# Twelve consecutive tokens per partition instead of every 128th: a new on-chip token order for a fused attention and MLP kernel

## The chip, the cores and the metric

The kernel runs on one core of a Trainium2 chip. Times are device microseconds (us) of one execution. The profile of an execution gives its own span, from the first to the last instruction, and its granted TensorE clock.

## The reference

The inputs are `u` and `v` of shape (8, 3008, 256), `z` of shape (8, 3008, 64), and two weights, all in float32. What is computed, cut to what matters:

```python
scores = (1.0 / S) * np.matmul(z, z.transpose(0, 2, 1))   # per batch, S = 3008
attn = np.maximum(scores, 0.0) ** 2
x = (u * np.matmul(attn, v)).reshape(B * S, D)            # B = 8, D = 256
h = x @ w_in                                              # d_ff = 2048
out = (h * np.cos(h)) @ w_out                             # float32, (24064, 256)
```

There is no mask and no position: every token of a batch meets every other token of it. A kernel may therefore hold the tokens of a batch in any order on chip, as long as `z`, `v`, `u` and `out` use the same one.

## The kernel before

**Tiles.** A batch of 3008 tokens is 23 blocks of 128 tokens and a tail of 64. Six groups (`NC = 6`) of four blocks make the unit of work, a *slot*; there are 8 x 6 = 48 slots. The blocks also fall into two halves of 12 blocks (`halves`), the second being 11 full blocks and the tail. Block `k` has its token number `p` on partition `p`: partition `p` holds tokens `p`, `128 + p`, `256 + p` and so on.

**Loads.** `load_z` brings half a batch of `z` into `z16` with a cast to fp16, twice side by side (`h` = 0, 1; lines 118 and 124). `load_rows` (line 140, and line 146 for the tail) brings four blocks of `v` or `u` with a cast to fp16. These are issued from GpSimd (POOL). For batch 0, `z` comes in float32 through six DMAs issued from SyncE and ScalarE (line 633, tail 639), is cast on VectorE and GpSimd (`cast_z`, line 645), turned on TensorE (`turn_on_pe`, line 649) and copied to `zT` (`copy_turned`). For the later batches, `turn_z` (line 133), and for every slot `turn_u` (line 160), turn the tiles by a transposing DMA on SyncE's queue. Weights come by two more GpSimd DMAs (lines 708 and 712).

**Work of a slot.** `phase_a(s)` multiplies the 24 score blocks by `v` (`emit_value`, line 258), in halves of the width: 23 blocks with `dh = 0`, the tail, 23 blocks with `dh = 1`; block `k` reads `vs[b, k // 4]`. Scores of later slots are made in between (`emit_score`, line 194), pass ScalarE (line 204) and VectorE (lines 209, 212), and their mirror images are made by transposing DMAs on SyncE's queue (`emit_turns`, lines 238 and 244). `gate_mul` (line 286) multiplies by `uT`. `phase_b(s)` alternates the first MLP product of slot `s - 1` (`emit_h`, line 404; cosine on ScalarE, line 412; product on VectorE, line 415) with the second one of slot `s - 2` (`product`, line 482, for all but the first and last slot; sums on GpSimd, lines 433, 434, 504, 507).

**Stores.** `store_half` writes two blocks of `out` with one DMA on SyncE's queue (line 547; lines 543 to 545 where the tails of two batches share a block). `last_y` makes the last slot's output block by block (line 525), copies it on ScalarE (line 572) and stores it (lines 578, 580, 581).

**Order.** The program is in `manual_schedule`: every engine executes in the order of the Python code. Batch `b + 1` has its `v` group 0 loaded in the slot `J = 4` of batch `b`, and groups 1 to 5 in the slot `J = 5`, after that slot's `phase_a`, since `v` has seven buffers and the last pass over the old groups must be done. At the start, seven matmuls on zeros (line 664) run before the first `z` block is turned.

Of the kernel before, what the change touches and what calls it, by code (L numbers as in the profile page):

```python
# [14 lines left out]
def kernel(  # L15
# [9 lines left out]
    nc = tc.nc  # L25
# [3 lines left out]
    B, S, D = u.shape  # L29
    dqk = z.shape[2]  # L30
    Dff = moe_w_in.shape[1]
    P = 128
    H = P // 2
    CW = 512
    NB = (S + P - 1) // P
    NC = (S + CW - 1) // CW
    WL = S - (NC - 1) * CW
    NFT = Dff // P
    NSLOT = B * NC
    NPC = 18  # L40
    assert D == 2 * P and dqk == H and S - (NB - 1) * P == H and NB == 4 * NC
    assert B % 2 == 0 and WL == 3 * P + H and NFT == 16

    inv_s2 = (1.0 / float(S)) * (1.0 / float(S))
    half_pi = float(math.pi / 2.0)
# [62 lines left out]
    halves = [(0, NB // 2), (NB // 2, NB)]  # L108
    z16s, zTs, vs, u16s, uTs, xs, gs = {}, {}, {}, {}, {}, {}, {}
    yps = {}  # L110

    def load_z(b, half):
        lo, hi = halves[half]
        z16 = zpool.tile([P, NB // 2, P], FP16, name="z16")
        z16s[b] = z16
        full = min(hi, NB - 1)
        for h in range(2):
            nc.gpsimd.dma_start(
                z16[:, 0:full - lo, h * dqk:(h + 1) * dqk],
                z[b, lo * P:full * P, :].rearrange("(j p) d -> p j d", p=P),  # L120
            )
            if hi == NB:
                for r in range(2):
                    nc.gpsimd.dma_start(
                        z16[r * H:(r + 1) * H, hi - lo - 1, h * dqk:(h + 1) * dqk],
                        z[b, (NB - 1) * P:S, :],
                    )
# [10 lines left out]
    def load_rows(t, src, b, g):  # L138
        full = 4 if g < NC - 1 else 3
        nc.gpsimd.dma_start(  # L140
            t[:, 0:full, :],
            src[b, g * CW:g * CW + full * P, :].rearrange("(j p) d -> p j d", p=P),
        )
        if full == 3:
            for r in range(2):
                nc.gpsimd.dma_start(t[r * H:(r + 1) * H, 3, :], src[b, S - H:S, :])

    def load_v(b, g):
        t = vpool.tile([P, 4, D], FP16, name="v16")
        load_rows(t, v, b, g)  # L150
        vs[b, g] = t

    def load_u(s):
        t = upool.tile([P, 4, D], FP16, name="u16")
        load_rows(t, u, s // NC, s % NC)
        u16s[s] = t
# [237 lines left out]
    def mwidth(m):  # L394
        return 3 * P if m % (2 * NC) == NC - 1 else CW
# [27 lines left out]
    T = 2 * P  # L423
# [41 lines left out]
    def product(m, n, place):  # L465
# [34 lines left out]
        if n in (1, 5):  # L500
            nc.scalar.activation(parts[n], acc, AF.Copy, bias=0.0, scale=inv_s2)
        elif n == 6:
            add(parts[6], parts[1])
            nc.gpsimd.tensor_tensor(c12, parts[6], parts[5], ALU.add)
        elif n == 7:
            add(c21, parts[6])
            nc.gpsimd.tensor_tensor(c22, c21, parts[5], ALU.add)
        elif n == 2:
            add(c11, parts[1])
        elif n == 3:  # L510
            add(c12, c12)
            store_half(m, 0, y_outs[m][0])
        else:
            add(c21, c21)
            store_half(m, 1, y_outs[m][1])

    def y_bank(m, k):
        if m == NSLOT - 1 and k == 3:
            return E[0][:, 0, 0:D]
        bank = 1 - k // 2 if m == NSLOT - 1 else k // 2  # L520
        return M[bank][:, (k % 2) * D:(k % 2 + 1) * D]

    def y_block(m, ft, k):
        final = m == NSLOT - 1
        nc.tensor.matmul(  # L525
            y_bank(m, k),
            gs[m][:, ft, k * P:(k + 1) * P],
            w_out16[:, ft, :],
            start=(ft == 0 and (k % 2 == 0 or (final and k == 3))),
            stop=(ft == NFT - 1 and (k % 2 == 1 or k == mwidth(m) // P - 1 or (final and k == 2))),  # L530
        )

    def emit_y(m, i):
        for ft in range(2 * i, 2 * i + 2):
            for k in range(mwidth(m) // P):
                y_block(m, ft, k)

    def store_half(m, half, o):
        b, J = m // NC, m % NC
        n = min(2, mwidth(m) // P - 2 * half)  # L540
        t0 = b * S + J * CW + half * T
        if J == NC - 1 and half == 1 and n == 2:
            nc.sync.dma_start(out[t0:t0 + P, :], o[:, 0, :])
            nc.sync.dma_start(out[t0 + P:t0 + P + H, :], o[0:H, 1, :])
            nc.sync.dma_start(out[b * S - H:b * S, :], o[H:P, 1, :])
        else:
            nc.sync.dma_start(
                out[t0:t0 + n * P, :].rearrange("(k p) d -> p k d", p=P), o[:, 0:n, :]
            )

    def store_y(m):
        for half in range(2):
            n = min(2, mwidth(m) // P - 2 * half)
            o = opool.tile([P, 2, D], FP32, name="o")
            nc.scalar.activation(
                o[:, 0:n, :],
                M[half].rearrange("p (k d) -> p k d", d=D)[:, 0:n, :],
                AF.Copy, bias=0.0, scale=inv_s2,
            )
            store_half(m, half, o)  # L560

    def last_y(m):
        b, J = m // NC, m % NC
        for ft in range(NFT):
            y_block(m, ft, 0)
            y_block(m, ft, 1)
        for k in range(4):
            if k >= 2:
                for ft in range(NFT):
                    y_block(m, ft, k)  # L570
            o = opool.tile([P, 2, D], FP32, name="o")
            nc.scalar.activation(
                o[:, 0, :], y_bank(m, k),
                AF.Copy, bias=0.0, scale=inv_s2,
            )
            t0 = b * S + J * CW + k * P
            if k < 3:
                nc.sync.dma_start(out[t0:t0 + P, :], o[:, 0, :])
            else:
                nc.sync.dma_start(out[t0:t0 + H, :], o[0:H, 0, :])  # L580
                nc.scalar.dma_start(out[b * S - H:b * S, :], o[H:P, 0, :])

    def phase_b(s):
# [46 lines left out]
    for g in range(NC):  # L630
        eng = nc.sync if g % 2 == 0 else nc.scalar
        full = 4 if g < NC - 1 else 3
        eng.dma_start(
            z32[g][:, 0:full, :],
            z[0, g * CW:g * CW + full * P, :].rearrange("(j p) d -> p j d", p=P),
        )
        if full == 3:
            for r in range(2):
                nc.sync.dma_start(z32[g][r * H:(r + 1) * H, 3, :], z[0, S - H:S, :])
# [78 lines left out]
    turn_u(3)  # L718
    load_u(4)
    load_z(1, 0)  # L720
    mix_weights()
    phase_b(2)
    turn_z(1, 0)
    load_z(1, 1)
    turn_u(4)

    for s in range(3, NSLOT + 1):
        b, J = s // NC, s % NC
        if s < NSLOT - 2:
            load_u(s + 2)  # L730
        if b > 0 and J == 2 and b + 1 < B:
            load_z(b + 1, 1)
        if s < NSLOT:
            phase_a(s)
        if b + 1 < B:
            if b > 0 and J == 0:
                load_z(b + 1, 0)
            if b > 0 and J == 1:
                turn_z(b + 1, 0)
            if J == (2 if b > 0 else 3):  # L740
                turn_z(b + 1, 1)
            if J == NC - 2:
                load_v(b + 1, 0)
            if J == NC - 1:
                for g in range(1, NC):
                    load_v(b + 1, g)
        if s < NSLOT - 2:
            turn_u(s + 2)
        phase_b(s)
    last_y(NSLOT - 1)  # L750


# [28 lines left out]
```

## Time and profile before

| What | us |
|---|---|
| Median of 3 runs (1192.8 to 1193.27) | 1193.12 |
| The profiled execution's own time | 1193.15 |
| Its span | 1191.4 |
| TensorE busy | 1183.3 |
| VectorE busy | 1012.3 |
| ScalarE busy | 794.9 |
| GpSimd busy | 690.5 |

A busy figure counts instructions in execution; for TensorE it includes the modelled overlap of pipelined matmuls. The queue that GpSimd fills ("software") carried 97440 packets and 32.78 MB and took 27.3% of 16 DMA engines' span; the queue of SyncE ("hardware", q1) carried 380752 packets and 112.93 MB and took 54.4%. In all there were 479862 packets, 404208 of them under 512 B. The granted clock was 0.999 of full speed. A line such as "v<-in_v_dram POOLq DMA_DIRECT2D x40, 256.0 KB, 8.8" reads: 40 DMAs of 256 KB each, with a median of 8.8 us from issue to landing.

### The profile page before, as it was taken

How to read it: one execution, taken by the hardware profiler on the slowest of the kernel's cores; microseconds unless marked ns; L12 is line 12 of the kernel's file. 1: busy time of each engine (PE TensorE's matmuls, PEld its weight loads, DVE VectorE, ACT ScalarE, POOL GpSimd, SP SyncE). 2: the span in 40 equal slices, each digit the busy share in tenths (PEclk: the TensorE clock that was granted, in tenths of full speed). 3: DMA queues.
4: the chain of work that ended last, by engine and by line, in shares of the span. 5: the costliest groups of instructions: out<-in, count | busy, mean ns of one | idle time of the engine just before them, and what ended most of it. 6: DMA issues, size and time to landing. Idle time of an engine off the chain costs nothing.

```text
span 1191.4 us, 29044 instructions
## 1 busy us (share of the span) xinstructions
PE 1183.3 (99%) x11887; PEld 727.2 (61%) x11887; DVE 1012.3 (85%) x1302; ACT 794.9 (67%) x927; POOL 690.5 (58%) x717
## 2 busy tenths in 40 slices
PE   9999999999999999999999999999999999999998
PEld 4556665665566656666566665656666566665566
DVE  6899888889988898888988889888888888888776
ACT  7966676667666676667676676666766666666454
POOL 3287746657466573755647556476565665545452
PEclk9999999999999999999999999999999999999999
DMA  9999998569995699946999459973898737964301
GB/s 160 172 170 163 138 147 131 102 121 134 143 130 98 123 140 162 131 84 104 157 147 135 85 104 161 169 119 72 122 164 149 122 71 123 166 125 86 65 20 54
DMA packets 479862, 148.00 MB, mean 124 GB/s; under 512 B 404208, under 2 KB 479472, under 8 KB 479728
## 3 DMA queue, kind: packets, MB, share of 16 engines
q1 hardware_dynamic: 380752, 112.93, 54.4%
q0 software_dynamic: 97440, 32.78, 27.3%
q8 instruction: 93, 1.52, 0.5%
q10 hardware_dynamic: 1536, 0.43, 0.2%
q14 instruction: 41, 0.34, 0.1%
HBM read 66.32 MB, written 24.64 MB: 76 GB/s over the span
## 4 chain that ended last, share of the span: by engine, by line
PE 97%; ACT 1%; DVE 1%; issue 0%; POOL 0%; DVEq 0%; ACTq 0%
PE E L404 27%; PE M L482 23%; PE M L258 20%; PE E L258 19%; PE E L194 5%; PE M L525 1%; ACT r L204 1%; PE M L460 1%; DVE g L415 0%; PE E L664 0%; DVE sm L270 0%; PE E L525 0%; POOL s L433 0%; ACT c L412 0%; DVE o L495 0%
## 5 line engine op out<-in xcount | busy, mean ns | idle before, releaser
L412 ACT ACTIVATE c<-E 128x1024 f16<-128x1024 f32 (+1 forms) x384 | 385.7, 1007 | 216.4 <-PE E L404 214.1
L415 DVE SCALAR_TENSOR_TENSOR g<-E,c 128x1024 f16<-128x1024 f32 (+1 forms) x384 | 458.4, 1195 | 60.6 <-ACT c L412 59.5
L204 ACT ACTIVATE r<-E 128x512 f16<-128x512 f32 (+1 forms) x342 | 327.9, 967 | 112.7 <-PE E L194 106.5
L258 PEld LDWEIGHTS <-v 64*128 64x128 f16 x4512 | 246.3, 94 | 229.3 <-issue 19.4
L404 PE MATMUL E<-x,w_in 128*128 128x512 f16 (+1 forms) x1408 | 354.0, 375 | 0.0
L433 POOL TENSOR_TENSOR s<-g 128x512 f16<-128x512 f16 (+1 forms) x184 | 208.3, 1132 | 188.5 <-DVE g L415 138.7
L258 PE MATMUL M<-A,v 64*128 64x512 f16 (+1 forms) x2256 | 283.0, 372 | 0.2 <-DVE o L495 0.2
L258 PE MATMUL E<-A,v 64*128 64x512 f16 (+1 forms) x2256 | 278.1, 371 | 0.0
L434 POOL TENSOR_TENSOR g<-g 128x512 f16<-128x512 f16 (+1 forms) x184 | 219.5, 1193 | 14.4
L404 PEld LDWEIGHTS <-w_in 128*128 128x128 f16 x1536 | 133.1, 98 | 108.9 <-issue 19.5
L482 PEld LDWEIGHTS <-g 128*128 128x128 f16 x2816 | 172.5, 98 | 40.8
L209 DVE TENSOR_TENSOR A<-r 128x1024 f16<-128x1024 f16 x240 | 174.0, 737 | 15.0 <-ACT r L204 14.3
L286 POOL TENSOR_TENSOR x<-sm,uT 128x512 f16<-128x512 f32 (+1 forms) x43 | 48.6, 1132 | 212.9 <-DVE sm L270 212.5
L482 PEld LDWEIGHTS <-s 128*128 128x128 f16 x2112 | 129.4, 98 | 32.1 <-DVE s L440 0.5
L194 PE MATMUL E<-zT 64*128 64x512 f16 (+4 forms) x684 | 127.6, 355 | 2.0 <-DVE sm L270 0.7
L440 DVE TENSOR_TENSOR s<-s,g 128x1024 f16<-128x1024 f16 (+1 forms) x92 | 100.6, 1094 | 2.1 <-POOL s L433 2.1
L482 PE MATMUL M<-w_mix,s 128*128 128x128 f16 x1408 | 94.0, 219 | 0.3 <-POOL s L433 0.3
L482 PE MATMUL M<-w_mix,g 128*128 128x128 f16 x1408 | 93.6, 219 | 0.0
L482 PE MATMUL M<-w_out,g 128*128 128x128 f16 x1408 | 93.6, 219 | 0.0
L212 DVE TENSOR_TENSOR A<-r 128x512 f16<-128x512 f16 (+1 forms) x102 | 79.6, 781 | 8.9 <-ACT r L204 8.1
L194 PEld LDWEIGHTS <-zT 64*128 64x128 f16 x684 | 38.8, 94 | 38.5 <-issue 4.0
L442 DVE TENSOR_TENSOR s<-g,s 128x1024 f16<-128x1024 f16 (+1 forms) x92 | 60.5, 660 | 0.0
(58 smaller groups left out, 646.9 us busy)
## 6 DMA issues: line engine op xcount, KB each, us to landing
out_dram<-o SPq DMA_DIRECT2D x87, 256.0 KB, 2.2
v<-in_v_dram POOLq DMA_DIRECT2D x40, 256.0 KB, 8.8
u<-in_u_dram POOLq DMA_DIRECT2D x40, 256.0 KB, 4.8
A<-A SPq DMA_TRANSPOSE x252, 5.1
z<-in_z_dram POOLq DMA_DIRECT2D x14, 192.0 KB, 10.6
z<-in_z_dram POOLq DMA_DIRECT2D x14, 176.0 KB, 5.9
v<-in_v_dram POOLq DMA_DIRECT2D x8, 192.0 KB, 11.9
u<-in_u_dram POOLq DMA_DIRECT2D x8, 192.0 KB, 4.1
```

Source lines behind the costliest of these rows:

```text
L194: nc.tensor.matmul(e[:, t, 0:Wt], zT[rows, k * P:(k + 1) * P], zT[rows, J * CW:J * CW + Wt], start=True, stop=True,)
L204: nc.scalar.activation(r[:, :, 0:W], e[:, :, 0:W], AF.Relu)
L209: nc.vector.tensor_tensor(a4, r4, r4, ALU.mult)
L212: nc.vector.tensor_tensor(a4, r[:, :, 0:W], r[:, :, 0:W], ALU.mult)
L258: nc.tensor.matmul(bank[:, 0:width(J)], vs[b, k // 4][t * H:(t + 1) * H, k % 4, dh * P:(dh + 1) * P], value_rhs(b, J, k, t), start=start, ...
L404: nc.tensor.matmul(e[:, f, 0:W], w_in16[:, k, ft * P:(ft + 1) * P], x[:, k, 0:W], start=(k == 0), stop=(k == 1),)
L412: nc.scalar.activation(c[:, :, 0:W], e[:, :, 0:W], AF.Sin, bias=half_pi, scale=inv_s2)
L415: return lambda: nc.vector.scalar_tensor_tensor(gs[m][:, 2 * i:2 * i + 2, 0:W], e[:, :, 0:W], 1.0, c[:, :, 0:W], ALU.mult, ALU.mult)
L433: nc.gpsimd.tensor_tensor(s1[:, f, 0:n], g[:, f, low], g[:, lower, low], ALU.add)
L434: nc.gpsimd.tensor_tensor(g[:, f, low], g[:, f, up], g[:, f, low], ALU.subtract)
L440: nc.vector.tensor_tensor(s2[:, f, 0:n], s1[:, f, 0:n], g[:, f, up], ALU.subtract)
L482: nc.tensor.matmul(acc[:, k * P:(k + 1) * P], left[:, ft, k * P:(k + 1) * P], right[:, ft, :], start=(ft == 0 and k == 0), stop=(ft == F - ...
```

## The change

The order of the tokens on chip changes within each half of a batch. The first half's 1536 tokens lie twelve to a partition: partition `p` holds tokens `12 p` to `12 p + 11`, and block `k` is the `k`-th of these on every partition. The second half's 1408 tokens lie eleven to a partition, and the tail of 64 stays as it was. `z`, `v`, `u` and `out` all follow the new order through two helpers. The number of DMAs, their bytes, the tiles in SBUF and every compute instruction stay the same; the address patterns on the DRAM side differ. In DRAM, a partition's four blocks of `v` or `u` are now 4 KB in one piece (3 KB in the last group), the twelve of `z` 3 KB, the four of batch 0's `z` 1 KB, and two blocks of `out` 2 KB. Where `last_y` stores one block, its 128 rows of 1 KB were adjacent and now stand 11 KB apart; the stores of tails are the same.

```diff
-    assert B % 2 == 0 and WL == 3 * P + H and NFT == 16
+    assert NC == 6 and B % 2 == 0 and WL == 3 * P + H and NFT == 16
...
+    def half_rows(rows, half):
+        lo, hi = halves[half]
+        n = min(hi, NB - 1) - lo
+        return rows[lo * P:(lo + n) * P, :].rearrange("(p j) d -> p j d", p=P)
+
+    def group_rows(rows, g):
+        first = 4 * (g % 3)
+        return half_rows(rows, g // 3)[:, first:first + (4 if g < NC - 1 else 3), :]
+
     def load_z(b, half):
...
-                z16[:, 0:full - lo, h * dqk:(h + 1) * dqk],
-                z[b, lo * P:full * P, :].rearrange("(j p) d -> p j d", p=P),
+                z16[:, 0:n, h * dqk:(h + 1) * dqk], half_rows(z[b], half)
...
     def load_rows(t, src, b, g):
         nc.gpsimd.dma_start(
             t[:, 0:full, :],
-            src[b, g * CW:g * CW + full * P, :].rearrange("(j p) d -> p j d", p=P),
+            group_rows(src[b], g),
         )
...
+    def out_rows(m):
+        b, J = m // NC, m % NC
+        return group_rows(out[b * S:(b + 1) * S, :], J)
+
     def store_half(m, half, o):
...
-            nc.sync.dma_start(out[t0:t0 + P, :], o[:, 0, :])
-            nc.sync.dma_start(out[t0 + P:t0 + P + H, :], o[0:H, 1, :])
+            nc.sync.dma_start(rows[:, 2, :], o[:, 0, :])
+            nc.sync.dma_start(out[(b + 1) * S - H:(b + 1) * S, :], o[0:H, 1, :])
             nc.sync.dma_start(out[b * S - H:b * S, :], o[H:P, 1, :])
         else:
-            nc.sync.dma_start(
-                out[t0:t0 + n * P, :].rearrange("(k p) d -> p k d", p=P), o[:, 0:n, :]
-            )
+            nc.sync.dma_start(rows[:, 2 * half:2 * half + n, :], o[:, 0:n, :])
...
     def last_y(m):
             if k < 3:
-                nc.sync.dma_start(out[t0:t0 + P, :], o[:, 0, :])
+                nc.sync.dma_start(out_rows(m)[:, k, :], o[:, 0, :])
             else:
-                nc.sync.dma_start(out[t0:t0 + H, :], o[0:H, 0, :])
+                nc.sync.dma_start(out[(b + 1) * S - H:(b + 1) * S, :], o[0:H, 0, :])
...
         eng.dma_start(
             z32[g][:, 0:full, :],
-            z[0, g * CW:g * CW + full * P, :].rearrange("(j p) d -> p j d", p=P),
+            group_rows(z[0], g),
         )
```

More of the change, by code (lines that the diff above doesn't have):

```diff
@@ L115, in load_z @@
         z16s[b] = z16
-        full = min(hi, NB - 1)
+        n = min(hi, NB - 1) - lo
         for h in range(2):
             nc.gpsimd.dma_start(
-                z16[:, 0:full - lo, h * dqk:(h + 1) * dqk],
-                z[b, lo * P:full * P, :].rearrange("(j p) d -> p j d", p=P),
+                z16[:, 0:n, h * dqk:(h + 1) * dqk], half_rows(z[b], half)
             )
@@ L536, in emit_y @@
                 y_block(m, ft, k)
+    def out_rows(m):
+        b, J = m // NC, m % NC
+        return group_rows(out[b * S:(b + 1) * S, :], J)
     def store_half(m, half, o):
-        b, J = m // NC, m % NC
+        b = m // NC
+        rows = out_rows(m)
         n = min(2, mwidth(m) // P - 2 * half)
-        t0 = b * S + J * CW + half * T
-        if J == NC - 1 and half == 1 and n == 2:
-            nc.sync.dma_start(out[t0:t0 + P, :], o[:, 0, :])
-            nc.sync.dma_start(out[t0 + P:t0 + P + H, :], o[0:H, 1, :])
+        if m % NC == NC - 1 and half == 1 and n == 2:
+            nc.sync.dma_start(rows[:, 2, :], o[:, 0, :])
+            nc.sync.dma_start(out[(b + 1) * S - H:(b + 1) * S, :], o[0:H, 1, :])
             nc.sync.dma_start(out[b * S - H:b * S, :], o[H:P, 1, :])
         else:
-            nc.sync.dma_start(
-                out[t0:t0 + n * P, :].rearrange("(k p) d -> p k d", p=P), o[:, 0:n, :]
-            )
+            nc.sync.dma_start(rows[:, 2 * half:2 * half + n, :], o[:, 0:n, :])
     def store_y(m):
@@ L575, in last_y @@
             )
-            t0 = b * S + J * CW + k * P
             if k < 3:
-                nc.sync.dma_start(out[t0:t0 + P, :], o[:, 0, :])
+                nc.sync.dma_start(out_rows(m)[:, k, :], o[:, 0, :])
             else:
-                nc.sync.dma_start(out[t0:t0 + H, :], o[0:H, 0, :])
+                nc.sync.dma_start(out[(b + 1) * S - H:(b + 1) * S, :], o[0:H, 0, :])
                 nc.scalar.dma_start(out[b * S - H:b * S, :], o[H:P, 0, :])
```

## The prediction

> **What bounds the kernel now.** I read the page's busy table and slices first:
>
> ```profile
> PE 1183.3 (99%) x11887; PEld 727.2 (61%) x11887; DVE 1012.3 (85%) x1302; ACT 794.9 (67%) x927; POOL 690.5 (58%) x717
> ...
> PE   9999999999999999999999999999999999999998
> ...
> DMA  9999998569995699946999459973898737964301
> ```
>
> TensorE (PE) is never short of work, and the DMA engines, at nine tenths in many slices, are not idle either. A busy PE need not be a PE at its peak, so the chain of work that ended last comes next:
>
> ```profile
> PE 97%; ACT 1%; DVE 1%; issue 0%; POOL 0%; DVEq 0%; ACTq 0%
> PE E L404 27%; PE M L482 23%; PE M L258 20%; PE E L258 19%; PE E L194 5%; PE M L525 1%; ACT r L204 1%; PE M L460 1%; DVE g L415 0%; PE E L664 0%; DVE sm L270 0%; PE E L525 0%; POOL s L433 0%; ACT c L412 0%; DVE o L495 0%
> ```
>
> 97% of the end time is matmuls one after the other; no DMA stands in it. In the chain's pieces, 8 matmuls of line 404 take 1.73 us (216 ns each) and 16 of line 258 the same 1.73 us (216 ns for a pair on the two 64-row halves). The waits of PE alone, all eight of them:
>
> ```profile
> PE E L664 <- DVE s L627: 1.2, 1, 1.2
> PE E L194 <- DVE sm L270: 0.7, 1, 0.7
> PE E L194 <- DVE g L415: 0.4, 1, 0.4
> PE E L194 <- ACT zT L657: 0.4, 1, 0.4
> PE M L482 <- POOL s L433: 0.3, 1, 0.3
> PE E L194 <- DVE zT L659: 0.2, 1, 0.2
> PE M L258 <- DVE o L495: 0.2, 1, 0.2
> PE E L194 <- ACT r L204: 0.2, 1, 0.2
> ```
>
> They sum to 3.6 us and none was ended by a DMA. So I forecast from three places where a transfer could still reach the end: the start-up, the tightest load of the interior, and the last stores.
>
> **What the Trainium skill says.** "TensorE: Matmul & The Clock Gate", section "Back-to-back issue gap", gives N/2.4 + 2.5 ns for one matmul at full clock: 216 ns for 512 columns. The trace agrees (216 ns), so PE streams at its rate and earlier data can't speed it up. "DMA: Bandwidth & Descriptors", section "Specifications", asks for rows of at least 512 B, and "Why small descriptors are slow (HBM only)" names a fixed cost per packet; the two weight loads, equal in bytes, point that way:
>
> ```profile
> w_in<-in_moe_w_in_dram POOLq DMA_DIRECT2D x1, 1024.0 KB, 11.0
> w_out<-in_moe_w_out_dram POOLq DMA_DIRECT2D x1, 1024.0 KB, 14.9
> ```
>
> The first moves in rows of 8 KB, the second in rows of 1 KB; what ran beside them differs, so it is a hint only. "Issuing engines are not separate DMA queues" says that all queues share the 16 engines. The trace agrees: two transposes of line 244 issued at 273.09 us, beside the loads of `v`, kept SyncE's queue 12.45 us, while three at 323.83, with few loads about, took 8.40.
>
> **The change, part by part.** No compute instruction and no DMA is added or taken away: 11887 matmuls at the same durations. What changes is how a DMA is cut.
>
> *Packets.* I expect one packet for each piece that is contiguous on both sides. A load of `v` or `u` goes from 512 packets (128 partitions x 4) to 128; with the 8 shorter ones of each tensor, 47104 rows become 12288. Two-block stores go from 256 to 128 (87 x 128 = 11136 fewer). Batch 0's `z` loses 2208. The later `z` keeps its 128-byte pieces, because its destination has gaps. 479862 packets become about 431700, and GpSimd's queue goes from 97440 to about 62600. The transposes, most of q1, stay.
>
> *Issue on POOL.* 96 loads at 751 to 817 ns (line 140). The nearest rows with fewer pieces are the tail loads (64 pieces, about 550 ns) and `w_in` (256 pieces, 751 ns), so each is worth 0 to 0.27 us, at most 26 us of POOL. POOL is 58% busy and in the steady part PE waits for it once, 0.3 us: priced at 0, up to -0.3 if that wait goes. Cover: VectorE's 85% and PE's own stream.
>
> *Start-up.* The first six loads of `z` land in 3.7 to 6.4 us. With 1 KB rows, I take 1 us less. The chain's start says what that is worth:
>
> ```profile
> 0.86 0.28 DVE s L627
> 1.14 0.04 issue
> 1.19 3.17 PE E L664 x7
> 4.35 0.04 issue
> 4.39 0.52 PE turned L649 x4
> ```
>
> VectorE has the first `z` at 3.91 and ends its cast at about 4.31, but PE is busy with seven matmuls on zeros until 4.36 and takes up the block at 4.39. At most 0.03 us can go there; what is late next is the zeros' end, which doesn't move. The later casts end at 5.97, 8.23 and 9.24 us, and PE reaches those blocks in its own order at 6.35, 9.61 and 11.13, after work that waits for ScalarE. Earlier casts bring nothing; they may cost something, since GpSimd's casts and issues slide under other VectorE work. Bounds: -0.3 to +0.3 us; I take -0.1.
>
> *Loads in the interior.* The tightest is `v` of the last batch, five big loads and two tails:
>
> ```profile
> L140 POOL DMA_DIRECT2D v<-in_v_dram x5: 740/742/746, 1007.2 to 1011.3; - x5
> L146 POOL DMA_DIRECT2D v<-in_v_dram x2: 539/548/558, 1012.1 to 1012.6; - x2
> ...
> DMA to landing us min/median/max: 11.1/15.4/16.1
> ```
>
> Group 5, the last big one, is issued at 1011.3 and lands 16.1 us later, at 1027.4. PE starts the slot's value products at 1024.17 and reaches block 20, group 5's first, after 40 matmuls and three score pairs, at 1029.15. That is a margin of 1.7 us. The same sum gives 3.6 us for batch 4 (tails), 4.1 for batch 2, 4.4 for batch 6, and over 7 for the odd batches. Earlier landing widens these margins and moves PE by 0. `z` and `u` have more: `u` is turned two slots ahead. The transposes of scores are queued on SyncE behind `u`'s and `z`'s turns; I matched the order of emission to the queue, and those near the `v` burst (285.68 to 289.66, line 238) serve a slot a whole 24.5 us later. Gain 0.
>
> *Stores.* Issue on SyncE's queue is 345 to 372 ns either way; 2.2 us to landing may fall. They wait for VectorE, nobody but the last slot waits for them. There, ScalarE waits 1.5 us for two stores to free a buffer, but its last copy starts at 1187.10, 0.04 us after PE's last matmul, so that wait is covered. The final two stores are tails and unchanged. The three single-block stores keep 128 packets of 1 KB, now 11 KB apart instead of adjacent; the trace has no such store. Bounds: 0, since the last (issued 1186.2, some 1.7 us to land) ends before the tails' 1189.7, to +1 us if scattered rows took twice as long. I take 0.
>
> *Sum:* 1193.15 (this execution, 0.03 above the median) - 0.1 + 0 + 0 + 0, about **1193.0**.
>
> **The rivals.**
>
> *Slower, the burst of `v` lands later.* One mechanism: GpSimd's loads and SyncE's transposes share the engines, which show nines throughout the burst; if 4 KB pieces from partitions 12 KB apart are served worse (fewer pieces in flight, or a poorer spread over HBM), PE stalls at block 20. With a delay d the loss is what d exceeds of 1.7, 3.6, 4.1 and 4.4 us, summed. It decides from d = 3.9 us (2.2 + 0.3 = 2.5 us, 1195.6); d = 6 gives 4.3 + 2.4 + 1.9 + 1.6 = 10.2 us, 1203.3. For it: engines full, a margin of 1.7. Against: `w_in`, and a quarter as many pieces.
>
> *Faster, transfers bound the ends after all.* The first `z` 1 us earlier would have to carry through start-up, and the 1.5 us of ScalarE's waits at the end would have to count: 2.5 us, 1190.6. Against: zeros until 4.36, and the last copy behind PE.
>
> *The cut doesn't change.* If the DMAs are still cut into rows as before, packets stay at 479862 and the time at 1193.1 with a slightly different DRAM order. This is no different in sign from the forecast.
>
> **How the numbers follow.** About 0.2% (2.4 us) is what a measurement of this kernel can tell from no change. My forecast gets 0.75, the uncut rival 0.11, both inside it: same 0.86. The later burst gets 0.09, the faster ends 0.05. In the same-cases the start-up bounds, the stores and the run-to-run spread (1192.8 to 1193.27) give about 1192 to 1194.6; the range reaches on towards both other cases, 1191.2 to 1195.0.
>
> **What the profile after would show.** Right: about 431700 packets, `v` in the interior landing well under 10 us, a lower share for q0, PE's waits the same eight within 0.5 us, the chain at 97% PE, zeros until 4.36 and the first turn at 4.39. Wrong: any wait of PE on a DMA or on `v`; a first turn before 4.3; a longer gap after 1187; a matmul with another duration.

## The result and the profile after

The change made the kernel slower: 1219.4 us (median of four runs, 1218.14 to 1220.22) against 1193.19 us, a ratio of 1.0218 with a 95% interval of 1.02 to 1.0236. The profiled execution took 1219.31 us and its span is 1217.5 us, 26.1 us more than the span before. The helpers are new, so line numbers have moved: `emit_value` is line 266 (was 258), `product` 490 (482), `load_rows` 148 and 154 (140 and 146), `emit_turns` 246 and 252 (238 and 244).

The chain of work that ended last, from the page of the changed kernel:

```profile
PE 84%; DMA 12%; DVE 1%; ACT 1%; issue 1%; POOL 0%; SPq 0%; DVEq 0%; ACTq 0%
PE E L412 23%; PE M L490 18%; PE M L266 18%; PE E L266 18%; DMA v<-in_v_dram 10%; PE E L202 5%; DMA out_dram<-o 1%; PE M L533 1%; ACT r L212 1%; PE M L468 1%; DVE g L423 1%; PE E L673 0%; DVE sm L278 0%; ACT c L420 0%; DVE A L217 0%
```

97% matmuls have become 84%, and loads of `v` stand in the chain with 10%. One piece of it, at the border of the first two batches (start, length):

```profile
130.32 0.28 issue
130.60 22.59 DMA v<-in_v_dram
153.19 0.04 issue
153.23 0.39 PE M L266 x2
```

A load of `v` issued at 130.60 us landed 22.59 us later, and two matmuls of line 266 started at once. The chain follows the late load instead of the 22 us of matmuls beside it; the time lost is only what PE waited. From the list of PE's waits (in all, times, longest), the three largest and one more:

```profile
PE M L266 <- DMA v<-in_v_dram: 14.1, 14, 3.5
PE M L490 <- issue: 3.2, 1, 3.2
PE M L490 <- DVE o L503: 1.6, 2, 1.2
...
PE M L266 <- DVE o L503: 0.8, 2, 0.5
```

The first line is new: 14 waits on `v`. All waits of PE sum to 23.4 us, 19.8 more than the 3.6 before; PE's busy time rose by 5.9 us (1183.3 to 1189.2) with the same 11887 matmuls, which I take to be modelled ends that stretch where a stream is broken (at the third border twelve matmuls of line 266 show 2.48 us instead of the usual 1.46). Together that is 25.7 of the 26.1 us. The single wait of 3.2 us put down to "issue" stays unexplained. It lies within the fifth burst, at 746.7 us, and that border is the only one with no wait on `v`.

The loss comes in portions. The first load of `v`'s burst starts at 127.8 us in the first batch and at 1030.9 in the last one, 903.1 us apart; before it was 128.4 and 1007.2, 878.8 apart. That is 24.3 us over six bursts, 4 us each on average (from one burst's start to the next, between 1.2 and 6.6 us are lost), and the seventh adds some 2 us. The last burst, to be held against the one shown before, by `v`'s tile and then PE's order of time:

```profile
L148 POOL DMA_DIRECT2D v<-in_v_dram x5: 528/531/531, 1030.9 to 1034.4; - x5
L154 POOL DMA_DIRECT2D v<-in_v_dram x2: 532/537/542, 1034.9 to 1035.4; - x2
...
DMA to landing us min/median/max: 18.0/19.9/20.3
```

```profile
1047.82 1.70 PE L266 MATMUL M<-A,v 64*128 64x512 f16 x12
1049.35 0.38 PE L202 MATMUL E<-zT 64*128 64x512 f16 x2
1049.57 0.60 PE L266 MATMUL M<-A,v 64*128 64x512 f16 x4
1050.47 1.04 PE L266 MATMUL M<-A,v 64*128 64x512 f16 x8 [0.30 <-DMA v<-in_v_dram]
1051.34 0.38 PE L202 MATMUL E<-zT 64*128 64x512 f16 x2
1052.57 1.04 PE L266 MATMUL M<-A,v 64*128 64x512 f16 x8 [0.85 <-DMA v<-in_v_dram]
1053.79 0.39 PE L266 MATMUL M<-A,v 64*128 64x512 f16 x2 [0.19 <-DMA v<-in_v_dram]
1054.02 0.38 PE L202 MATMUL E<-zT 64*128 64x512 f16 x2
1054.23 1.24 PE L266 MATMUL M<-A,v 64*128 64x512 f16 x10
```

Two matmuls of line 266 make one block, so the three waits stand ahead of blocks 8, 12 and 16, the first ones of groups 2, 3 and 4. The prediction's slower rival had put the stall at block 20. There PE doesn't wait: after the earlier waits it reaches that block at about 1054.9 us, and group 5 is in by 1034.4 + 20.3 = 1054.7. The other borders are alike: the waits on `v` stand ahead of blocks 4, 8, 12 or 16, none ahead of block 20. The packets and landings, from the DMA part of the page:

```profile
DMA packets 431734, 148.00 MB, mean 122 GB/s; under 512 B 401264, under 2 KB 409968, under 8 KB 431600
...
q0 software_dynamic: 62624, 32.78, 26.9%
...
v<-in_v_dram POOLq DMA_DIRECT2D x40, 256.0 KB, 18.9
u<-in_u_dram POOLq DMA_DIRECT2D x40, 256.0 KB, 4.5
```

The cut is as announced, and `u` lands sooner than before (4.8 us). But `v`, at the same size, goes from 8.8 to 18.9 us. The other party is on SyncE's queue. At the first border, before and after (start, time on the queue):

```profile
128.18 10.10 SPq L244 DMA_TRANSPOSE A<-A  x2
```

```profile
127.60 25.87 SPq L252 DMA_TRANSPOSE A<-A  x2
```

The two transposes of scores issued beside the burst take 2.5 times as long. Both sides lose, so neither takes the engines from the other: in the 26 us from 127 on, this core moved 4.11 MB before and 2.29 MB after, while the engines are shown as nine tenths busy in 30 of the 40 slices of that stretch before and in 32 after.

### The profile page after: what moved, and what is told of

Its sections match the earlier page's. It is cut to its first block, busy times and chain, and to the rows that moved or that the text cites. A ratio compares the mean times of both kernels' runs of the same rounds, so it can differ in the third digit from the quotient of the medians.

```text
span 1217.5 us, 29044 instructions
## 1 busy us (share of the span) xinstructions
PE 1189.2 (98%) x11887; PEld 727.3 (60%) x11887; DVE 1005.0 (83%) x1302; ACT 794.9 (65%) x927; POOL 666.7 (55%) x717
## 2 busy tenths in 40 slices
DMA packets 431734, 148.00 MB, mean 122 GB/s; under 512 B 401264, under 2 KB 409968, under 8 KB 431600
## 3 DMA queue, kind: packets, MB, share of 16 engines
q0 software_dynamic: 62624, 32.78, 26.9%
## 4 chain that ended last, share of the span: by engine, by line
PE 84%; DMA 12%; DVE 1%; ACT 1%; issue 1%; POOL 0%; SPq 0%; DVEq 0%; ACTq 0%
PE E L412 23%; PE M L490 18%; PE M L266 18%; PE E L266 18%; DMA v<-in_v_dram 10%; PE E L202 5%; DMA out_dram<-o 1%; PE M L533 1%; ACT r L212 1%; PE M L468 1%; DVE g L423 1%; PE E L673 0%; DVE sm L278 0%; ACT c L420 0%; DVE A L217 0%
## 5 line engine op out<-in xcount | busy, mean ns | idle before, releaser
L266 PE MATMUL M<-A,v 64*128 64x512 f16 (+1 forms) x2256 | 286.9, 373 | 15.1 <-DMA v<-in_v_dram 14.1
L217 DVE TENSOR_TENSOR A<-r 128x1024 f16<-128x1024 f16 x240 | 170.9, 722 | 36.7 <-ACT r L212 35.7
L448 DVE TENSOR_TENSOR s<-s,g 128x1024 f16<-128x1024 f16 (+1 forms) x92 | 95.9, 1043 | 2.1 <-POOL s L441 2.1
## 6 DMA issues: line engine op xcount, KB each, us to landing
v<-in_v_dram POOLq DMA_DIRECT2D x40, 256.0 KB, 18.9
```

Of the source, the lines that this page charges most:

```text
L217: nc.vector.tensor_tensor(a4, r4, r4, ALU.mult)
L266: nc.tensor.matmul(bank[:, 0:width(J)], vs[b, k // 4][t * H:(t + 1) * H, k % 4, dh * P:(dh + 1) * P], value_rhs(b, J, k, t), start=start, ...
L448: nc.vector.tensor_tensor(s2[:, f, 0:n], s1[:, f, 0:n], g[:, f, up], ALU.subtract)
```

## The experiments

Landings of `v` are medians over the 40 loads of 256 KB, and "the two transposes" are those at the first border, unless said otherwise. A ratio is to the kernel before, as timed beside the run.

### Is it the length of the pieces, or the order in DRAM?

**Gaps in the `v` tile.** 32 bytes of gap behind every row keep the DMA from joining rows:

```diff
-        t = vpool.tile([P, 4, D], FP16, name="v16")
+        t = vpool.tile([P, 4, D + 16], FP16, name="v16")[:, :, 0:D]
```

> The changed kernel with 32 bytes of gap behind each 512-byte row of the v tile in SBUF, so that a load of v is cut into four pieces of 512 B per partition again, from the same DRAM addresses 12 KB apart. Theory A (2 KB pieces of v and the transposes of scores hold each other up on shared DMA engines): v lands in 9 to 11 us in the interior, the two transposes at the burst take 12 to 14 us of SyncE's queue, no wait of PE on v, 1192 to 1194 us. Rival B (the DRAM order, 12 KB from partition to partition, is what is served slowly): v stays at about 19 us and the time at 1215 to 1222 us. Rival C (z, u or out in the new order cause it): 1219 us as well, with v's landing back at 10 us.

Measured: 1193.46 us, ratio 1.0 (0.9991 to 1.0009); `v` landed in 10.8 us and the two transposes took 13.00 us. Everything else in the new order stayed. The whole loss is gone with the length of `v`'s pieces, which speaks for theory A and against B and C.

**Gaps after every second row**, pieces of 1 KB:

```diff
+        t = vpool.tile([P, 2, 2 * D + 16], FP16, name="v16")[:, :, 0:2 * D]
...
+                t.rearrange("p a (k d) -> p a k d", d=D), rows.rearrange("p (a k) d -> p a k d", k=2)
```

> The changed kernel with the gap after every second row of the v tile: pieces of 1 KB (group 5, with three full blocks, takes two DMAs instead of one). Theory A: in between, v landing in 12 to 16 us, the burst's two transposes 15 to 19 us, and since the margins at block 20 are 1.7 to over 7 us, 1196 to 1206 us. Rival B: 1215 to 1222 us.

Measured: 12.6 us for `v`, 16.16 us for the transposes, both as expected; but 1193.0 us, ratio 0.9999 (0.9991 to 1.0008), not the 1196 us or more. In its trace PE has no wait on `v`: the margins held.

**Gaps inside a row**, pieces of 256 B:

```diff
+        t = vpool.tile([P, 4, 2, P + 8], FP16, name="v16")[:, :, :, 0:P]
...
```

> The changed kernel with gaps of 16 bytes behind every 256 bytes of the v tile, so v moves in pieces of 256 B. Theory A, that a piece holds up the transposes for its own length: the burst's two transposes take no longer than with 512 B (13 us at the first batch), v lands in 10 to 16 us,[...] and the time is 1192 to 1195 us.

Measured: `v` 9.8 us, the transposes 11.41 us, 1193.67 us (1.0009, 1.0001 to 1.0016). The landing is a little below the 10 to 16 us expected, the rest as expected. The transposes of the kernels with 256 B, 512 B and 1 KB, in turn:

```profile
128.12 11.41 SPq L260 DMA_TRANSPOSE A<-A  x2
127.82 13.00 SPq L252 DMA_TRANSPOSE A<-A  x2
127.62 16.16 SPq L262 DMA_TRANSPOSE A<-A  x2
```

With the change they make a series, all in the new order with `u` in pieces of 2 KB:

| Pieces of `v` | two transposes, us | `v` landing, us | ratio to before |
|---|---|---|---|
| 256 B | 11.41 | 9.8 | 1.0009 |
| 512 B | 13.00 | 10.8 | 1.0 |
| 1 KB | 16.16 | 12.6 | 0.9999 |
| 2 KB (the change) | 25.87 | 18.9 | 1.0218 |

At equal bytes a longer piece also means fewer pieces, so the series can't tell length from number. The gap also moves the rows in SBUF; a gap that leaves pieces of 2 KB was not run.

**`v` alone in the new order**, from the kernel before (`True` selects the change's `group_rows`, whose copy is left out here):

```diff
-        load_rows(t, v, b, g)
+        load_rows(t, v, b, g, True)
```

> The kernel before with v alone loaded in the new order (its tokens then no longer match those of z, so the sums are over mismatched pairs; every instruction and size is that of the kernel before). Theory A and rival B: v lands in 19 to 21 us in the interior, PE waits on v in each batch, 1215 to 1222 us. Rival C: 1193 us.

Measured: 1197.38 us (1195.14 to 1201.58), ratio 1.0033 (1.0015 to 1.0051). Nobody had expected this: `v` alone costs some 4 us of the 26. In its profile `v` lands in 13.6 us, with medians between 11.8 and 21.3 us from one border to the next.

**`v` dense**, four tokens to a partition within a group, so partitions stand 4 KB apart:

```diff
-            src[b, g * CW:g * CW + full * P, :].rearrange("(j p) d -> p j d", p=P),
+            src[b, g * CW:g * CW + full * P, :].rearrange(
+                "(p j) d -> p j d" if src is v else "(j p) d -> p j d", p=P
+            ),
```

> The kernel before with v alone loaded four consecutive tokens to a partition within its group of 512 (tokens no longer match those of z): the same 2 KB pieces in SBUF and 4 KB in DRAM as in the change, but a load reads one contiguous stretch of 512 KB and the partitions stand 4 KB apart. Theory A: as slow as the change, 1215 to 1222 us, v landing in 19 to 21 us. Rival B: 1192 to 1195 us, v in 10 us or less.

Measured: 1198.57 us, ratio 1.0037 (1.0021 to 1.0053), `v` 13.1 us. Both numbers missed, but the comparison holds: with the partitions 4 KB apart it costs as much as with 12 KB (1.0033). Together with the gaps, which keep the 12 KB and cost nothing, the order of `v` in DRAM is out.

### What else does it take?

**`v` and `u` in the new order**, from the kernel before; and its counterpart, the change with `u` in the old order:

```diff
-        load_rows(t, u, s // NC, s % NC)
+        load_rows(t, u, s // NC, s % NC, True)
```

> The kernel before with v and u in the new order (z and out in the old one, so tokens are mismatched; instructions and sizes as before). v alone gave 1197 us and landings of 12 to 21 us that differ from batch to batch; the change gave 1219 us. Theory A1 (the load of u, issued 1.5 us ahead of v's burst, adds more 2 KB pieces to the same collision): landings of 19 to 22 us in every batch, 1212 to 1222 us. Theory A2 (the stores of out add it): 1195 to 1200 us.

```diff
-            group_rows(src[b], g),
+            group_rows(src[b], g) if src is v else
+            src[b, g * CW:g * CW + full * P, :].rearrange("(j p) d -> p j d", p=P),
```

> The changed kernel with u alone loaded in the old order (u's tokens then don't match those of the product it gates), so that u moves in pieces of 512 B and v in pieces of 2 KB. Theory A1: 1195 to 1200 us, as with v alone. Theory A2: 1215 to 1222 us.

Measured: 1216.69 us with both (1212.25 to 1228.8; ratio 1.0211, 1.0153 to 1.0269), at landings whose medians per border are 17.6 to 22.2 us; 1197.38 us with `u` old (1.0042, 1.0025 to 1.0059). So `u` takes a cost of 4 us to one of 23, though TensorE never waits for `u`. Theory A1 stands as far as the load of `u` goes. Whether it is the length of `u`'s pieces or their order in DRAM that counts is not shown, since no run kept `u`'s new order with short pieces. The pause put down to "issue" comes back in the run with both, again in the fifth burst, with 5.1 us.

**`v` and `out`**, from the kernel before, with `out_rows` and the stores of the change:

```diff
-        load_rows(t, v, b, g)
+        load_rows(t, v, b, g, True)
...
-                out[t0:t0 + n * P, :].rearrange("(k p) d -> p k d", p=P), o[:, 0:n, :]
+            nc.sync.dma_start(rows[:, 2 * half:2 * half + n, :], o[:, 0:n, :])
```

> The kernel before with v and out in the new order (z and u in the old one, tokens mismatched). Theory A1: 1195 to 1200 us, as with v alone. Theory A2: 1212 to 1222 us.

Measured: 1199.23 us, ratio 1.0044 (1.0033 to 1.0056), runs from 1194.64 to 1208.0. That agrees with `v` alone; the stores are not the cause.

### Does it need the transposes?

**Transposes later**, in the change and in the kernel before:

```diff
                 emit_score()
-                emit_turns(divmod(s + 1, NC), 1)
+                emit_turns(divmod(s + 1, NC), 0 if J == NC - 1 else 1)
...
-            if i in (1, 3, 5):
+            if i in ((5, 6, 7) if s % NC == NC - 1 else (1, 3, 5)):
```

> The changed kernel with the transposes of scores moved off the burst of v: in the last slot of a batch none is issued during the value products, and the three of that slot are issued behind the sixth to eighth MLP unit of phase_b, some 5 us later than v's last load. All pieces and addresses are those of the change. Theory A (large pieces and transposes hold each other up): v lands in 5 to 8 us, no wait of PE on v, 1192 to 1195 us. If large pieces were slow by themselves in the interior, v stays at 15 to 20 us and the time above 1205 us.

> The kernel before (pieces of 512 B) with the transposes moved off the burst of v as in the run on the change. With that run's 5.7 us for 2 KB pieces it tells what the piece size is worth when nothing collides. Theory A: v lands in 5 to 8 us, a little later than with 2 KB pieces; 1192 to 1194 us.

Measured: 1192.79 us from the change (0.9998, 0.9989 to 1.0007) and 1193.39 us from the kernel before (1.0, 0.9992 to 1.0009). The 40 loads land in 5.7 and 6.1 us. All landings of `v`, first of the change with later transposes, then of the kernel before with them:

```profile
DMA to landing us min/median/max: 4.0/6.0/7.1
```

```profile
DMA to landing us min/median/max: 4.2/6.2/7.7
```

Nothing is above 7.7 us in either. Without the transposes beside them, 2 KB pieces land about as soon as 512 B (5.7 against 6.1 us, one profile of each); beside them they take 18.9 us against 8.8. With the loads out of the way the transposes take 3.7 us each (six of line 252 in 22.08 us, in the changed kernel with later transposes) where the change has two in 25.87. Neither the pieces nor the transposes are slow, only the two together.

### What is `u`'s part?

**`u` behind `v`**, the change with one move in the last slot of a batch:

```diff
+        u_late = J == NC - 1 and b + 1 < B
-        if s < NSLOT - 2:
+        if s < NSLOT - 2 and not u_late:
             load_u(s + 2)
...
                     load_v(b + 1, g)
+        if s < NSLOT - 2 and u_late:
+            load_u(s + 2)
```

> The changed kernel with one move: in the last slot of a batch the load of u is issued behind the loads of v instead of ahead of them. All pieces are those of the change. If u matters because its 2 KB pieces stand at the head of the queue when the transposes begin: 1195 to 1201 us, as with u in the old order. If it matters by its bytes in large pieces anywhere in the burst: 1212 to 1222 us.

Measured: 1193.46 us, ratio 1.0006 (0.9998 to 1.0013). It is better than either number: the same 2 KB pieces of `u` and `v` in the same burst cost nothing, with `v` at 8.8 us. At the first border, SyncE's queue:

```profile
127.80 15.74 SPq L252 DMA_TRANSPOSE A<-A  x2
```

**Transposes 2 us later**, from the change:

```diff
                 emit_score()
-                emit_turns(divmod(s + 1, NC), 1)
+                if J < NC - 1:
+                    emit_turns(divmod(s + 1, NC), 1)
+                elif i == max(at):
+                    turns[:3] = turns[:3][::-1]
+                    emit_turns((0, 0), 3)
```

> The changed kernel with the three mirror images of a batch's last slot issued together behind that slot's last score, in reverse order, so that the transposes start some 4 us later, when u has landed and several loads of v in 2 KB pieces are on their way. Theory S (what is in flight when the transposes start sets the two out of step): v's last loads land in 15 to 22 us, the transposes take over 20 us, 1200 to 1222 us. Theory Q (the amount of large pieces queued from the transposes' start on): fewer are left than in the change, so v lands in 7 to 11 us and the time is 1192 to 1195 us.

The transposes began only 2 us later, when loads of `v` were on their way:

```profile
129.61 14.75 SPq L252 DMA_TRANSPOSE A<-A  x2
```

Measured: 1193.45 us, ratio 1.0 (0.9991 to 1.0009), `v` 6.2 us. The last loads of a burst were later than expected under theory Q (12.6 us for the shorter ones of group 5). Over the seven borders the two transposes took 14.75 to 18.40 us, not over 20. So theory S failed: large pieces in flight when the transposes start are not enough for the collapse. The test was narrower than planned, though: at 129.61 us the load of `u`, issued at 126.54 and 4.7 us on its way, had not landed, and only two loads of `v` had been issued.

Theory Q forecast the time, but the run before speaks against it: with `u` behind `v`, the first load of `v` is issued at 128.05 us, after the transposes' start at 127.80, so that all of `v` and `u` is queued from that start on, and nothing was lost. The amount alone is not the rule. What the runs show is narrower: the collapse at every border came only with `u` and `v` both in the new order, `u` issued ahead of `v`, and the transposes started between the two; moving any one of these removed most or all of it. Why two microseconds suffice, and what happens inside a DMA engine, is open; so is whether the 4 KB read or the 2 KB written is the length that matters, since the gaps cut both.

## Why the prediction was wrong

**The step that failed** is "Loads in the interior": "Earlier landing widens these margins and moves PE by 0". The landing did not become earlier; that term, priced at 0, measured about +26 us. It rested on the Trainium skill, "DMA: Bandwidth & Descriptors", section "Why small descriptors are slow (HBM only)", and on `w_in` against `w_out`. For a load by itself the direction is right, if small (5.7 against 6.1 us), but the burst was shown in the prediction as lying beside the transposes, and for a load beside them the series runs the other way. The two lines compared told nothing of that: neither load was picked for what ran beside it. That both queues share the engines was said, with 12.45 us for two transposes as evidence, and no price was put on the length of a piece in that shared queue.

**The slower rival** had the burst, the sharing with the transposes and the order of size, and got 0.09. Its sum comes near: taking for each border the largest landing after, less the largest before, less the margin, gives for the first 23.0 - 11.1 - 7.4 = 4.5 us and for the seven 4.5 + 3.5 + 4.5 + 2.2 + 1.7 + 4.6 + 2.5 = 23.5 us, against the 26.1 us that the span grew. In part that is luck. The stalls stood ahead of blocks 4 to 16 and not of block 20, and the fifth border, with 1.7 us in the sum, has no wait on `v` at all but the unexplained pause of 3.2 us. Of its two reasons, the spread over HBM with partitions 12 KB apart is ruled out for `v` by the dense `v` and the gaps. The other, fewer pieces in flight, can't be told from longer pieces by these runs. The weight was wrong: I held "a quarter as many pieces" against it, and that was what cost the time beside the transposes.

**The margins** were right as far as they went: with 1 KB pieces `v` lands at 14.7 us at the last border, under the 16.1 us of the kernel before, and no time is lost. They were worked out for group 5 alone; when the whole burst is late, PE is held up for groups 1 to 4 first.

**Packets**: predicted about 431700 and 62600, measured 431734 and 62624 (batch 0's `z` lost 2176 packets, not 2208). The rival of an unchanged cut is out.

**Issue on POOL**: the bound of 0 to 0.27 us each held. From the groups of the changed kernel:

```profile
L148 POOL DMA_DIRECT2D u<-in_u_dram x48 | 28.8, 599 | 1.1 <-issue 1.0
L148 POOL DMA_DIRECT2D v<-in_v_dram x48 | 25.8, 538 | 17.1 <-PE E L266 10.5 <-PE E L202 6.5
```

751 and 817 ns became 538 and 599. POOL's busy time fell by 23.8 us and PE gained nothing, as priced.

**Start-up**: the first loads of `z` landed in 2.9 us instead of 3.7, 0.8 less where I took 1. The term "at most 0.03 us" was mis-sized. In the chain of the changed kernel:

```profile
1.19 3.16 PE E L673 x7
4.35 0.24 PE turned L658 x4
...
5.68 1.95 ACT r L212 x2
```

In order of time PE took up the block at 4.15, not 4.39, while the zeros' modelled end stayed at 4.35, and ScalarE's first scores start at 5.68 instead of 6.01: 0.33 us. I had read a modelled end of pipelined matmuls as the moment at which PE becomes free.

**The stores**: 0, as taken. From ScalarE's last copy (1213.25) to the span's end are 4.25 us, against 4.30 before. The faster rival is out.

No version beat the kernel before: the later transposes (0.9998) and the 1 KB pieces (0.9999) can't be told from it, and in both PE is busy for all but 8 to 9 us of the span (1183.0 of 1192.2 and 1182.9 of 1190.8 us).

## What to carry to other kernels

Longer pieces made the loads of `v` no slower by themselves here, yet a burst of them beside transposing DMAs nearly halved what was moved (4.11 to 2.29 MB in 26 us); price a load by what shares the engines at that moment, not by its median over the kernel. When a change "only" makes transfers better, list the loads with the smallest margin and give their lateness a real chance, even where no wait on a DMA is in the profile. The remedies here cost nothing: shorter pieces by a gap in the tile, another order of issue, or transposes started two microseconds later.

## What the runs showed of the hardware

Two transposes beside a burst of loads took 11.41, 13.00, 16.16 and 25.87 us at the first border as the loads' pieces went from 256 B to 2 KB, at equal bytes. The last doubling costs far more than the ones before it, and they took that long at every border (20.77 to 25.87 us in the change) only while `u`, in the new order too, was queued ahead of the burst and the transposes started right behind it; with `u` behind, the same two took 15.74 us at the first border. In the collapse the DMA engines show as busy as ever while they move about half (88 GB/s instead of 158 in those 26 us): a busy share of DMA was no measure of progress.
